# A decode kernel of grouped-query attention and an MLP on one core: weight rows of 16 and 28 KiB, the last output-weight load moved between parts of w2, and w2's first part in two transfers of 119 and 9 partitions

## The chip, the core and the metric

The kernel runs on one core of one Trainium2 chip. The metric is device time in microseconds (us), of which the median of several executions counts. One further execution was recorded with the hardware profiler; its own time is given beside its span below.

## What is computed

For a batch of 8 single tokens of width 512, the block adds the token, an attention over a cache of 8192 positions (32 query heads, 8 key/value heads), and a two-layer MLP with the Mish activation. Both branches read the same layer-normed token.

```python
def _A_ref(x, k_cache, v_cache, wq, wo):
    ...
    q = (x @ wq).reshape(B, Sq, Hq, Dh).transpose(0, 2, 1, 3)
    ...
    scores = jnp.einsum("bhqd,bhkd->bhqk", q, k) * (Dh ** -0.5)
    p = _softmax(scores, axis=-1)
    o = jnp.einsum("bhqk,bhkd->bhqd", p, v)
    return o.transpose(0, 2, 1, 3).reshape(B, Sq, Hq * Dh) @ wo

def _B_ref(x, w1, b1, w2):
    h = jnp.einsum("bsd,df->bsf", x, w1) + b1
    ...
    return jnp.einsum("bsf,fd->bsd", act, w2)

xn = _layernorm(x, axis=-1)
return x + _A_ref(xn, A_k_cache, A_v_cache, A_wq, A_wo) + _B_ref(xn, B_w1, B_b1, B_w2)
```

All data is 32-bit floating point. The two caches are 64 loads of 4 MiB each; the weights are small beside them (wq 8 MiB, wo 8 MiB, w1 3.5 MiB, w2 3.5 MiB), and everything is read once.

## The kernel before

**The work.** The query heads are worked on in 16 packs `p` of 4 batch rows each; pack `p` belongs to key/value head `n = p // 2`. A pack has four items of keys and four of values, each with one 4 MiB load. `scores` (line 305) multiplies the queries of a pack with one key block, `maximum` and `weights` (346, 368) make the exponentials of a finished pack on ScalarE and VectorE, `values` (411) multiplies them with one value block, `merge` (442) turns the result into a column of `oT`.

**The list of items and the buffers.** Lines 630 to 647 write the work out as a list `items`: wq's first part, the keys of pack 0 with w1 between them, then keys of pack `p` and values of pack `p-1` in turn, with a part of wq or of wo now and then. Each item is a load and a generator of work. The loop at line 650 issues the load of item `i + 3` ahead of the work of item `i`. All loads go into four buffers of 32 KiB per partition (`buffer`, line 90) in rotation, so the load of item `i + 4` waits on the SyncE (SP) queue until all readers of item `i` are done. All loads are issued by SP, in list order.

**Late work.** `after(k, f)` (548) puts `f` off by `k` steps; a step (`step`, 551) is taken at each `yield` of an item's work. A key item yields four times, after 8 of its 32 matmul passes each; a value item twice; a wo item once (line 619), which is a step of its own. `merge` is put off by two steps after a value item, `outputs` (456) by three after the wo item that holds its weights. `exponents` (599) comes a step after `largest` (595). TensorE and VectorE run their instructions in the order in which the program writes them (line 663 on).

**The weights.** `load_blocks` (93) brings wq, wo and w1 with 4 KiB (wq, wo) or 3.5 KiB (w1) of contiguous memory for each row of a transfer, since each partition takes one row out of each block. `project` (235) makes the queries of two heads from a wq part, `outputs` the product of two finished heads with a wo part, which is added up over the four parts in `acc`, and `mish` (483) the whole first MLP layer. `load_w2` (130) brings w2 in three loads of 16, 8 and 4 KiB rows, each into a buffer of its own, and `down` (533) multiplies each.

**The end of the list.** The last items are the four value blocks of pack 15, wo's last part, and w2's three parts. After the last `down`, VectorE adds `acc` (line 659) and SP writes the result (660).

Of the kernel before, what the change touches and what calls it, by code (L numbers as in the profile page):

```python
# [13 lines left out]
P = 128  # L14
# [42 lines left out]
W = GK * NB // P  # L57
W4 = 4
TW = W // TG
W2R = G * FT // 2 * FP // P  # L60
FAR = 1e38

# [5 lines left out]
def kernel(  # L68
# [21 lines left out]
    def buffer():  # L90
        return kv.tile([P, NB * BW], F32, name="kv")

    def load_blocks(src, lo, n):

        _, rows, width = src.shape
        t = buffer()[:rows, : n * width].rearrange("p (j f) -> p j f", j=n)
        nc.sync.dma_start(t, src[lo : lo + n].rearrange("j p f -> p j f"))
        return t

    def batch_blocks(src, p, b):  # L100
# [2 lines left out]
        return src[lo : lo + NB]  # L103

    def load_batch(src, p, b):

        t = buffer()
        nc.sync.dma_start(
            t,
            batch_blocks(src, p, b)  # L110
            .rearrange("j p f -> (j p f)")
            .rearrange("(p f) -> p f", p=P),
        )
        return t

    def load_k(p, b):
        if p > 0:
# [7 lines left out]
        )  # L125
        return t

    w2_rows = w2.rearrange("j p f -> (j p) f").rearrange("(q i) f -> q (i f)", i=W2R)

    def load_w2(lo, hi):  # L130

        t = buffer()[:, : (hi - lo) * BW]
        nc.sync.dma_start(t, w2_rows[:, lo * BW : hi * BW])
        return t

    x_sb = const.tile([B, D], F32, name="x_sb")
    nc.scalar.dma_start(x_sb, x)
# [27 lines left out]
    far = const.tile([P, NH], F32, name="far")  # L165

    isel = const.tile([P, W4], F32, name="isel")
    qT = [const.tile([P, PB * (QB + 1)], F32, name=f"qT{i}") for i in range(QBUFS)]
    qc = const.tile([P, 4, KR, REP, B], F32, name="qc")
    qc0 = const.tile([P, KA, REP, B], F32, name="qc0")  # L170
    xnT = const.tile([P, CC, B], F32, name="xnT")
    acc = const.tile([P, P], F32, name="acc")
    aT = const.tile([P, 2 * W2R, Q], F32, name="aT")

    def setup():
        make_identity(nc, ident)
        nc.gpsimd.memset(ones, 1.0)
        for t in qT:
            nc.gpsimd.memset(t, 0.0)
        nc.vector.memset(M, 0.0)  # L180
        nc.vector.memset(H, 0.0)
        for o in O:
            nc.vector.memset(o, 0.0)
# [18 lines left out]
        nc.vector.tensor_scalar(xc, xc, st[:, 4:5], None, op0=ALU.mult)  # L202
        for c in range(CC):
            nc.tensor.transpose(  # L204
                M[:, c * B : (c + 1) * B], xc[:, c * P : (c + 1) * P], ident[:B, :B]
            )
        nc.vector.tensor_copy(xnT.rearrange("p c b -> p (c b)"), M[:, : CC * B])  # L207
# [5 lines left out]
        nc.vector.reduce_sum(bsel, ident.rearrange("p (j i) -> p j i", j=NB), axis=AX.X)  # L213
        nc.vector.reduce_sum(rsel, ident.rearrange("p (g r) -> p r g", g=G), axis=AX.X)
# [13 lines left out]
        nc.vector.reduce_sum(far, mine.rearrange("p h s -> p s h"), axis=AX.X)  # L228
        nc.vector.tensor_scalar(far, far, FAR, -FAR, op0=ALU.mult, op1=ALU.add)

    q_at = [H[:, 384:512], H[:, 256:384]]

    def project(n, w):

        for c in range(CC):
            for h in range(REP):
                lo = (n % 2 * REP + h) * DH
                nc.tensor.matmul(  # L240
                    q_at[n % 2][Q * h : Q * h + B, :],
                    xnT[:, c, :],
                    w[:, c, lo : lo + DH],
                    start=(c == 0),
                    stop=(c == CC - 1),
                )

    def spread_q(n, k, copies, dst):
# [188 lines left out]
                op1=ALU.add,  # L437
            )

    oT = {}  # L440

    def merge(p, b):

        n, hb = divmod(p, NP)
        at = 168 + b * REP
        nc.tensor.matmul(M[:, at : at + REP], OS.pop((p, b)), hsel, start=True, stop=True)  # L446
        if b == PB - 1:
            if hb == 0:
                oT[n] = work.tile([P, REP, B], F32, name="oT", bufs=4)
            nc.vector.tensor_mul(  # L450
                oT[n][:, :, hb * PB : (hb + 1) * PB],
                M[:, 168 : 168 + REP * PB].rearrange("p (b h) -> p h b", h=REP),
                RT.pop(p),
            )

    def outputs(n, w):

        if n == 0:

            for g in range(G):  # L460
                nc.tensor.matmul(
                    M[Q * g : Q * g + B, 256:384],
                    ident[:B, :B],
                    x_sb[:, g * P : (g + 1) * P],
                    start=True,
                    stop=False,
                )
        for h in range(2 * REP):
            for g in range(G):
                at = h % 2 * D + g * P  # L470
                nc.tensor.matmul(  # L471
                    M[Q * g : Q * g + B, 256:384],
                    oT[n + h // REP][:, h % REP, :],
                    w[:, h // 2, at : at + P],
                    start=(h == 0 and n > 0),
                    stop=(h == 2 * REP - 1),
                )
        if n == 0:
            nc.vector.tensor_copy(acc, M[:, 256:384])
        else:  # L480
            nc.vector.tensor_add(acc, M[:, 256:384], acc)

    def mish(w1_sb):

# [6 lines left out]
        for c in range(CC):  # L491
            for g in range(G):
                nc.tensor.matmul(
                    hp[Q * g : Q * g + B, :],
                    xnT[:, c, :],
                    w1_sb[:, c * 2 + g // 2, g % 2 * FG : (g % 2 + 1) * FG],
                    start=False,
                    stop=(c == CC - 1),
                )

        scratch = work.tile([P, TG, NH, P], F32, name="e", bufs=1).rearrange("p t s f -> p (t s f)")
# [29 lines left out]
        nc.vector.transpose(aT.rearrange("p j q -> p (j q)"), act)  # L531

    def down(lo, hi, w):
        for j in range(2 * lo, 2 * hi):
            for g in range(G):
                at = (j - 2 * lo) * D + g * P
                nc.tensor.matmul(
                    H[Q * g : Q * g + B, :P],
                    aT[:, j, :B],
# [19 lines left out]
    def wq_item(i):  # L559
# [17 lines left out]
                after(2, then)  # L577
            yield

        return lambda: load_blocks(wq, i * CC, CC), work_on  # L580

    def w1_work(t):
        mish(t)
# [39 lines left out]
    def w2_work(lo, hi):  # L623
        def work_on(t):
            down(lo, hi, t)
            yield

        return work_on

    setup()  # L630
    items.append(wq_item(0))
    for i in range(PB * PACKS + PB):
        p, b = divmod(i, PB)
        if p < PACKS:
# [1 line left out]
            if b == 2 and p % (2 * NP) == 2 and p < PACKS - NP:  # L636
                items.append(wq_item(p // (2 * NP) + 1))
            if i == 2:
                items.append((lambda: load_blocks(w1, 0, 2 * CC), w1_work))
# [74 lines left out]
```

## Time and profile before

| what | value |
|---|---|
| median of 3 executions | 1320.84 us (1320.44 to 1321.55) |
| time of the profiled execution | 1319.99 us |
| span of the profiled execution, first to last instruction | 1318.2 us |
| time outside that span | 1.8 us |
| mean granted TensorE clock | 0.973 |
| memory read | 561.01 MB |

The profile gives the busy time of each engine over the span. PE is TensorE's matmul, PEld its weight load, DVE VectorE, ACT ScalarE, POOL GpSimd, SP SyncE, which only issues transfers here. A matmul of this kernel's 32-bit data is two passes, and each pass is one record, so 32 matmuls appear as "x64". In the view of windows, the columns are the stretch in us, its length, the busy time and instruction count of PE, PEld, DVE, ACT and POOL, the granted clock, the mean busy share of the 16 DMA engines, and the rate in GB/s. A packet is counted where it ends, so short windows can show a share over 1. In the timeline, the columns are start, duration, engine, line and operation, tiles, and count, and at the end the idle time before with what ended it. L328 is line 328 of the kernel before.

### The profile page before, as it was taken

To read this page: it belongs to the slowest core of one execution; us is meant where nothing else is said; L and a number is where in the kernel's file an instruction comes from. 1 tells how busy PE (TensorE), PEld (TensorE's weight loads), DVE (VectorE), ACT (ScalarE), POOL (GpSimd) and SP (SyncE) were. 2 spreads that over 40 slices of the span, in tenths; PEclk is the share of its full clock that TensorE was granted. 3 is DMA by queue.
4 is the path that set the end of the run, shared out by engine and by line. 5 is a ranking of instruction groups with operands and counts; after the bars stand their busy time and mean duration, and the time that the engine had idled before them with its cause. 6 is when DMAs were issued, how large, how long until landed. Compare 5 with 4: busy or idle time off the path is not lost.

```text
span 1318.2 us, 11315 instructions
## 1 busy us (share of the span) xinstructions
PE 1196.0 (91%) x5100; PEld 512.6 (39%) x5100; DVE 268.6 (20%) x667; ACT 42.2 (3%) x71; POOL 8.7 (1%) x10
## 2 busy tenths in 40 slices
PE   4999989999979998999998999899999899999986
PEld 3333344433434434434333434444343343343322
DVE  5330311303021031120302112131120301202021
ACT  1000000000000000000000000000000000000000
POOL 2000000000000000000000000000000000000000
PEclk9999989999989998999998999899999899999988
DMA  9999999999999999999999999999999999999997
GB/s 385 433 432 432 431 429 429 429 429 430 433 426 432 433 425 431 431 433 430 432 432 427 432 431 425 433 428 430 432 431 425 426 435 433 428 432 429 429 433 310
DMA packets 24856, 561.81 MB, mean 426 GB/s; under 512 B 2268, under 2 KB 2400, under 8 KB 7656
## 3 DMA queue, kind: packets, MB, share of 16 engines
q1 hardware_dynamic: 24784, 561.06, 99.4%
q8 instruction: 40, 0.66, 0.2%
q14 instruction: 8, 0.07, 0.0%
q10 hardware_dynamic: 24, 0.02, 0.0%
HBM read 561.01 MB, written 0.07 MB: 426 GB/s over the span
## 4 chain that ended last, share of the span: by engine, by line
PE 53%; DMA 46%; DVE 1%; issue 0%; ACT 0%
DMA kv<-in_kT 42%; PE s L328 42%; PE o L419 6%; DMA kv<-in_v 2%; PE h L263 1%; DMA kv<-in_w 1%; PE s L315 1%; PE m L471 1%; DVE e L190 0%; PE m L446 0%; PE h L240 0%; DVE qs L253 0%; DMA x_sb<-in_x 0%; PE m L372 0%; DVE oT L450 0%
## 5 line engine op out<-in xcount | busy, mean ns | idle before, releaser
L328 PE MATMUL s<-kv,qT 128*128 128x512 f32 x1920 | 873.4, 609 | 75.9 <-DMA kv<-in_kT 75.9
L328 PEld LDWEIGHTS s<-kv,qT 128*128 128x128 f32 x1920 | 361.4, 194 | 525.6 <-issue 447.2
L419 PE MATMUL o<-kv,pt 128*32 128x512 f32 x2048 | 243.3, 610 | 12.5 <-DVE pt L391 6.3
L429 DVE TENSOR_SCALAR os<-o,isel 128x128 f32<-128x128 f32 x64 | 22.5, 351 | 595.1 <-PE o L419 595.1
L419 PEld LDWEIGHTS o<-kv,pt 128*32 128x32 f32 x2048 | 73.5, 139 | 157.8 <-issue 140.4
L382 ACT ACTIVATE e<-s,nms 128x1024 f32<-128x1024 f32 x32 | 35.4, 1110 | 1182.4 <-DVE nms L376 1182.4
L391 DVE STREAM_TRANSPOSE pt<-e 128x1024 f32<-128x1024 f32 x32 | 63.0, 2006 | 39.5 <-ACT e L382 39.5
L431 DVE SCALAR_TENSOR_TENSOR os<-o,isel,os 128x128 f32<-128x128 f32 x192 | 67.4, 351 | 6.8
L339 DVE TENSOR_REDUCE nm<-s 128x1 f32<-128x1024 f32 x16 | 19.6, 1225 | 206.3 <-PE s L328 204.8
L446 PEld LDWEIGHTS m<-hsel,os 128*128 128x128 f32 x128 | 23.8, 193 | 39.4 <-issue 30.0
L315 PE MATMUL s<-kv,qT 128*64 128x512 f32 x128 | 29.9, 625 | 1.6 <-issue 1.4
L288 DVE TENSOR_SCALAR qT<-qc,bsel 128x128 f32<-128x128 f32 x120 | 30.6, 341 | 0.0
L446 PE MATMUL m<-hsel,os 128*128 128x4 f32 x128 | 19.5, 223 | 6.5 <-DVE nr L350 4.9
L263 PE MATMUL h<-psel,qs 128*128 128x32 f32 x136 | 20.4, 309 | 4.0 <-DVE qs L253 4.0
L263 PEld LDWEIGHTS h<-psel,qs 128*128 128x128 f32 x136 | 20.4, 232 | 7.7 <-DVE qs L253 4.7
L315 PEld LDWEIGHTS s<-kv,qT 128*64 128x64 f32 x128 | 9.8, 145 | 20.8 <-issue 19.8
L270 DVE COPY qc<-h 128x256 f32<-128x256 f32 (+1 forms) x9 | 3.7, 410 | 56.1 <-PE h L263 56.1
L204 PE MATMUL m<-ident,e 8*128 8x8 f32 x4 | 0.6, 247 | 12.4 <-DVE e L202 12.4
L253 DVE TENSOR_SCALAR qs<-h 128x1024 f32<-128x1024 f32 (+1 forms) x9 | 10.4, 1160 | 2.9 <-PE h L240 2.9
L450 DVE TENSOR_TENSOR oT<-m,r 128x16 f32<-128x16 f32 x16 | 2.7, 171 | 36.4 <-PE m L446 36.4
L407 DVE RECIPROCAL r<-m 128x16 f32<-128x16 f32 x16 | 4.1, 257 | 29.1 <-PE m L403 29.1
L240 PE MATMUL h<-kv,xnT 128*8 128x128 f32 x256 | 9.4, 309 | 0.3 <-DVE xnT L207 0.3
(85 smaller groups left out, 127.3 us busy)
## 6 DMA issues: line engine op xcount, KB each, us to landing
kv<-in_kT SPq DMA_DIRECT2D x64, 4096.0 KB, 24.5
kv<-in_v SPq DMA_DIRECT2D x64, 4096.0 KB, 29.6
kv<-in_wq SPq DMA_DIRECT2D x4, 2048.0 KB, 19.3
kv<-in_wo SPq DMA_DIRECT2D x4, 2048.0 KB, 20.0
kv<-in_w SPq DMA_DIRECT2D x1, 3584.0 KB, 36.3
kv<-in_w SPq DMA_DIRECT2D x1, 2048.0 KB, 21.8
kv<-in_w SPq DMA_DIRECT2D x1, 1024.0 KB, 16.4
kv<-in_w SPq DMA_DIRECT2D x1, 512.0 KB, 7.1
```

Source lines behind the costliest of these rows:

```text
L263: nc.tensor.matmul(H[:, r * R : (r + 1) * R], qs[:, r].rearrange("p g i -> p (g i)"), psel.rearrange("p h b -> p (h b)"), start=True, stop ...
L288: nc.vector.tensor_scalar(t[:, :, :, lo : lo + R - U + 1 : U], q, bsel[:, j : j + 1], None, op0=ALU.mult)
L315: nc.tensor.matmul(sp[WK * z : WK * (z + 1), cols], t[:, w : w + WK], k[:, z, at : at + 512], start=(b == 0 and i == 0), stop=(b == PB - 1 ...
L328: nc.tensor.matmul(sp[:, cols], t[:, w : w + P], k[:, at : at + 512], start=(b == 0 and r == 0), stop=(b == PB - 1 and r == KR - 1),)
L339: nc.vector.tensor_reduce(NM[p], sp, axis=AX.X, op=ALU.max, negate=True)
L382: nc.scalar.activation(e[:, :, s, :], S[p % 2].rearrange("p (t f) -> p t f", t=TG), AF.Exp, bias=nms[:, s : s + 1], accum_out=l[:, s : s + 1],
L391: nc.vector.transpose(pt.rearrange("p (m t r) -> p t m r", m=TW, t=TG)[:, half * i : half * (i + 1)], e.rearrange("p t s (q m) -> p t m (s ...
L419: nc.tensor.matmul(o[Q * c : Q * (c + 1), :], PT[p][:, W4 * R * j + b : W4 * R * (j + 1) : PB], vt[:, 512 * j : 512 * (j + 1)], start=(k = ...
L429: nc.vector.tensor_scalar(os, o[:, :DH], isel[:, 0:1], None, op0=ALU.mult)
L431: nc.vector.scalar_tensor_tensor(os, o[:, DH * i : DH * (i + 1)], isel[:, i : i + 1], os, op0=ALU.mult, op1=ALU.add,)
L446: nc.tensor.matmul(M[:, at : at + REP], OS.pop((p, b)), hsel, start=True, stop=True)
L471: nc.tensor.matmul(M[Q * g : Q * g + B, 256:384], oT[n + h // REP][:, h % REP, :], w[:, h // 2, at : at + P], start=(h == 0 and n > 0), st ...
```

## The change

Six things are changed together.

1. wq, wo and w1 are read as one flat array cut into 128 rows, so that a partition takes 16 KiB (wq, wo) or 28 KiB (w1) of contiguous memory. The rows of the weights then stand on other partitions, and the other factor of each product is brought into the same order: for wq by a strided transpose of the normed token, for w1 by a widened copy `xw` made in the set-up (two VectorE copies, eight transposes, two masked copies), for wo by a new function `turn`, which picks every fourth row of `oT` with eight small matmuls and copies the result to `oW`.
2. `mish` has 8 instead of 4 rounds over the contraction, each of the same width.
3. A wo item other than the last takes no step of its own any more: `after(3, ...)` stands, but the `yield` behind it is gone.
4. w2 has one buffer for all its parts, which are 10, 14 and 4 KiB of each row (columns 0 to 5, 5 to 12, 12 to 14 in units of 2 KiB).
5. The first of these parts is two transfers, over partitions 0 to 118 and over 119 to 127.
6. wo's last load stands between w2's first and second part; its product is put off by one step only, adds into the same PSUM region as `down`, and needs no VectorE addition of its own.

```diff
+    def rows_of(blocks):
+        return blocks.rearrange("j p f -> (j p f)").rearrange("(p f) -> p f", p=P)
+    def load_rows(blocks):
+        src = rows_of(blocks)
+        t = buffer()[:, : src.shape[1]]
+        nc.sync.dma_start(t, src)
+        return t
...
+    W2_PARTS = ((0, 5), (5, 12), (12, 14))
+    FEW = 119
+    w2_sb = []
+    def load_w2(parts):
+        if not w2_sb:
+            w2_sb.append(buffer()[:, : W2R * BW])
+        for lo, hi in parts:
+            cols = slice(lo * D, hi * D)
+            for rows in [slice(0, FEW), slice(FEW, P)] if lo == 0 else [slice(0, P)]:
+                nc.sync.dma_start(w2_sb[0][rows, cols], rows_of(w2)[rows, cols])
+        return w2_sb[0]
...
+        wide = scratch[:B, 2 * D : 2 * D + W1R * P]
+        for t in range(2):
+            nc.vector.tensor_copy(
+                wide.rearrange("b (r c t i) -> b r c t i", r=W1R, c=CC, t=2)[:, :, :, t, :],
+                xc.rearrange("b (c i r) -> b r c i", c=CC, r=W1R),
+            )
+        for r in range(W1R):
+            nc.tensor.transpose(
+                M[:, 64 + r * B : 64 + (r + 1) * B], wide[:, r * P : (r + 1) * P], ident[:B, :B]
+            )
+        for t in range(2):
+            nc.vector.tensor_scalar(xw[:, :, t, :], ..., half[:, t : t + 1], None, op0=ALU.mult)
...
+            if hb == NP - 1:
+                after(1, lambda: turn(n))
+
+    def turn(n):
+        if n % 2 == 0:
+            oW[n] = work.tile([P, OR, 2, B], F32, name="oW")
+        to = oW[n - n % 2]
+        o = oT.pop(n)
+        for k in range(2):
+            j = n % 2 * 2 + k
+            for r in range(OR):
+                nc.tensor.matmul(
+                    M[Q * j : Q * (j + 1), 384 + r * 2 * B : 384 + (r + 1) * 2 * B],
+                    ident[:, r::OR],
+                    o[:, 2 * k : 2 * k + 2, :].rearrange("p h b -> p (h b)"),
+                    start=True, stop=True,
+                )
+        rows = slice(n % 2 * 64, n % 2 * 64 + 64)
+        nc.vector.tensor_copy(
+            to[rows].rearrange("p r h b -> p (r h b)"), M[rows, 384 : 384 + OR * 2 * B]
+        )
...
     def wo_work(n):
         def work_on(t):
-            after(3, lambda: outputs(n, t))
-            yield
+            if n == HKV - 2:
+                after(1, lambda: outputs(n, t))
+                yield
+            else:
+                after(3, lambda: outputs(n, t))
...
-            if i > PB and (i - PB + 1) % (2 * NP * PB) == 0:
-                n = (p - 1) // NP - 1
-                items.append((lambda n=n: load_blocks(wo, n * 2, 4), wo_work(n)))
-    for lo, hi in ((0, 4), (4, 6), (6, 7)):
-        items.append((lambda lo=lo, hi=hi: load_w2(lo, hi), w2_work(lo, hi)))
+            if i > PB and (i - PB + 1) % (2 * NP * PB) == 0 and p < PACKS:
+                items.append(wo_item((p - 1) // NP - 1))
+    for part in W2_PARTS:
+        items.append((lambda part=part: load_w2([part]), w2_work([part])))
+        if part is W2_PARTS[0]:
+            items.append(wo_item(HKV - 2))
```

`project`, `outputs`, `mish` and `down` index the loaded rows by round instead of by block; `project`, `outputs` and `down` keep their number of matmuls in all.

More of the change, by code (lines that the diff above doesn't have):

```diff
@@ L59 @@
 TW = W // TG
+QR = CC
+OR = 4
+W1R = 2 * CC * P // P
 W2R = G * FT // 2 * FP // P
@@ L105, in load_batch @@
     def load_batch(src, p, b):
[L107 to L114, printed above, removed]
+        return load_rows(batch_blocks(src, p, b))
     def load_k(p, b):
@@ L167 @@
     isel = const.tile([P, W4], F32, name="isel")
+    half = const.tile([P, 2], F32, name="half")
     qT = [const.tile([P, PB * (QB + 1)], F32, name=f"qT{i}") for i in range(QBUFS)]
@@ L170 @@
     qc0 = const.tile([P, KA, REP, B], F32, name="qc0")
[L171 removed]
+    xnT = const.tile([P, QR, B], F32, name="xnT")
+    xw = const.tile([P, W1R, 2, B], F32, name="xw")
     acc = const.tile([P, P], F32, name="acc")
@@ L202, in setup @@
         nc.vector.tensor_scalar(xc, xc, st[:, 4:5], None, op0=ALU.mult)
[L203 to L207, printed above, removed]
+        for r in range(QR):
+            nc.tensor.transpose(M[:, r * B : (r + 1) * B], xc[:, r::QR], ident[:B, :B])
+        nc.vector.tensor_copy(xnT.rearrange("p r b -> p (r b)"), M[:, : QR * B])
         nc.vector.tensor_copy(
@@ L229, in setup @@
         nc.vector.tensor_scalar(far, far, FAR, -FAR, op0=ALU.mult, op1=ALU.add)
+        wide = scratch[:B, 2 * D : 2 * D + W1R * P]
[9 more added lines that the diff above has]
+        for t in range(2):
+            nc.vector.tensor_scalar(
+                xw[:, :, t, :],
+                M[:, 64 : 64 + W1R * B].rearrange("p (r b) -> p r b", r=W1R),
+                half[:, t : t + 1],
+                None,
+                op0=ALU.mult,
+            )
     q_at = [H[:, 384:512], H[:, 256:384]]
     def project(n, w):
-        for c in range(CC):
+        for r in range(QR):
             for h in range(REP):
-                lo = (n % 2 * REP + h) * DH
+                at = r * BW + (n % 2 * REP + h) * DH
                 nc.tensor.matmul(
                     q_at[n % 2][Q * h : Q * h + B, :],
[L242 to L245, printed above, removed]
+                    xnT[:, r, :],
+                    w[:, at : at + DH],
+                    start=(r == 0),
+                    stop=(r == QR - 1),
                 )
@@ L454, in merge @@
             )
+            if hb == NP - 1:
[12 more added lines that the diff above has]
+                    o[:, 2 * k : 2 * k + 2, :].rearrange("p h b -> p (h b)"),
+                    start=True,
+                    stop=True,
+                )
+        rows = slice(n % 2 * 64, n % 2 * 64 + 64)
+        nc.vector.tensor_copy(
+            to[rows].rearrange("p r h b -> p (r h b)"), M[rows, 384 : 384 + OR * 2 * B]
+        )
     def outputs(n, w):
+        last = n == HKV - 2
+        to = H[:, :P] if last else M[:, 256:384]
         if n == 0:
@@ L467, in outputs @@
                 )
[L468 to L477, printed above, removed]
+        for r in range(OR):
+            for h in range(2):
+                for g in range(G):
+                    at = r * BW + h * D + g * P
+                    nc.tensor.matmul(
+                        to[Q * g : Q * g + B, :],
+                        oW[n][:, r, h, :],
+                        w[:, at : at + P],
+                        start=(r == 0 and h == 0 and 0 < n and not last),
+                        stop=(r == OR - 1 and h == 1 and not last),
+                    )
         if n == 0:
-            nc.vector.tensor_copy(acc, M[:, 256:384])
-        else:
-            nc.vector.tensor_add(acc, M[:, 256:384], acc)
+            nc.vector.tensor_copy(acc, to)
+        elif not last:
+            nc.vector.tensor_add(acc, to, acc)
     def mish(w1_sb):
@@ L490, in mish @@
             )
-        for c in range(CC):
+        for r in range(W1R):
             for g in range(G):
+                at = r * F // 2 + g % 2 * FG
                 nc.tensor.matmul(
                     hp[Q * g : Q * g + B, :],
-                    xnT[:, c, :],
-                    w1_sb[:, c * 2 + g // 2, g % 2 * FG : (g % 2 + 1) * FG],
+                    xw[:, r, g // 2, :],
+                    w1_sb[:, at : at + FG],
                     start=False,
-                    stop=(c == CC - 1),
+                    stop=(r == W1R - 1),
                 )
@@ L533, in down @@
     def down(lo, hi, w):
-        for j in range(2 * lo, 2 * hi):
+        for j in range(lo, hi):
             for g in range(G):
-                at = (j - 2 * lo) * D + g * P
+                at = j * D + g * P
                 nc.tensor.matmul(
@@ L617, in work_on, with w2_work, wo_item @@
         def work_on(t):
-            after(3, lambda: outputs(n, t))
-            yield
+            if n == HKV - 2:
[3 more added lines that the diff above has]
+                after(3, lambda: outputs(n, t))
         return work_on
-    def w2_work(lo, hi):
+    def w2_work(parts):
         def work_on(t):
-            down(lo, hi, t)
-            yield
-        return work_on
+            for lo, hi in parts:
+                down(lo, hi, t)
+                yield
+        return work_on
+    def wo_item(n):
+        return lambda: load_rows(wo[n * 2 : n * 2 + 4]), wo_work(n)
     setup()
```

20 lines of the change are left out of this document (6 added, 14 removed).

## The prediction, made before the change was run

> **What bounds the kernel now.** First the busy times and queues of the page.
>
> ```profile
> span 1318.2 us, 11315 instructions
> PE 1196.0 (91%) x5100; PEld 512.6 (39%) x5100; DVE 268.6 (20%) x667; ACT 42.2 (3%) x71; POOL 8.7 (1%) x10
> q1 hardware_dynamic: 24784, 561.06, 99.4%
> q8 instruction: 40, 0.66, 0.2%
> q10 hardware_dynamic: 24, 0.02, 0.0%
> ```
>
> SP's queue keeps the 16 DMA engines busy for 99.4% of the span: the stream of loads is the limit, PE's 91% is not. Only what shortens the stream, interrupts it, or stands behind its last byte counts. Next the windows of the stream and of its end.
>
> ```profile
> 29.50:36.00 6.50, 5.11 (x17) 2.01 (x18) 3.26 (x13) 0.00 (x0) 0.00 (x0) 1.00 1.03 406
> 39.50:55.50 16.00, 16.00 (x98) 4.98 (x96) 2.30 (x5) 1.86 (x2) 0.00 (x0) 1.00 1.01 429
> 174.50:177.50 3.00, 3.00 (x9) 1.33 (x8) 0.00 (x0) 0.00 (x0) 0.00 (x0) 1.00 1.02 410
> ...
> 1304.00:1305.00 1.00, 1.00 (x8) 0.17 (x4) 0.00 (x0) 0.00 (x0) 0.00 (x0) 0.62 1.03 430
> 1305.00:1306.50 1.50, 1.16 (x12) 0.14 (x4) 0.26 (x1) 0.00 (x0) 0.00 (x0) 1.00 0.56 235
> 1312.50:1313.00 0.50, 0.50 (x28) 0.50 (x20) 0.00 (x0) 0.00 (x0) 0.00 (x0) 1.00 0.19 74
> 1313.00:1314.00 1.00, 1.00 (x44) 1.00 (x40) 0.00 (x0) 0.00 (x0) 0.00 (x0) 1.00 0.00 0
> ```
>
> w1's 3.5 KiB rows come at 406 GB/s, wq's 4 KiB rows at 410, pack 0's 16 KiB rows at 429. At 1305.0 the busy share falls from 1 to 0.56: 9 engines work, 7 have run dry, about 1305.1. The last stops near 1312.9, having had w2's last 0.5 MB (1.3 us at 410 GB/s) to do, which the seven still lacked. So **seven engines are 1312.9 - 1.3 - 1305.1 = 6.5 us ahead** of the last. The instruction row fits: 40 packets of 16.5 KB at 0.2% of 16 x 1318 us are at least 1 us of an engine each; shared by nine they make 4.4 delays, 1.5 us each if they make the 6.5.
>
> Last the timeline behind the last value load.
>
> ```profile
> 1299.68 3.65 PE L419 MATMUL o<-kv,pt 128*32 128x512 f32 x16 [4.02 <-DMA kv<-in_v]
> 1303.77 2.38 PE L419 MATMUL o<-kv,pt 128*32 128x512 f32 x16
> ...
> 1308.22 0.17 DVE L450 TENSOR_TENSOR oT<-m,r 128x16 f32<-128x16 f32 x1 [0.48 <-PE m L446]
> 1309.68 1.93 PE L537 MATMUL h<-kv,aT 128*8 128x128 f32 x64 [1.49 <-DMA kv<-in_w]
> ...
> 1312.15 1.06 PE L537 MATMUL h<-kv,aT 128*8 128x128 f32 x32 [0.54 <-DMA kv<-in_w]
> ...
> 1313.02 1.93 PE L471 MATMUL m<-kv,oT 128*8 128x128 f32 x64
> ...
> 1314.77 0.62 PE L537 MATMUL h<-kv,aT 128*8 128x128 f32 x16
> ...
> 1315.46 0.29 DVE L659 TENSOR_TENSOR res<-h,acc 128x128 f32<-128x128 f32 x1
> ```
>
> PE starts on the last value block at 1299.68, 0.45 us behind its last byte (estimated from 1312.9 and the next start); call that byte X = 1299.2. The final addition starts 16.3 us after X, with `outputs` (1.75 us) standing behind the last load.
>
> **The change part by part**, against the profiled execution's 1319.99 us (span plus 1.8), which lies 0.85 under the median.
>
> *Rows.* 2.10 MB take 5.11 us at 410 GB/s and 4.89 at 429: 0.22 saved on each of seven loads ahead of X (wo's last is counted below), and w1's 3.67 MB 9.04 against 8.55. Together **-2.0**; rates of so short windows allow -1.3 to -2.6.
>
> *Set-up.* PE waits for the new transposes before `project`.
>
> ```profile
> 11.79 0.47 DVE L202 TENSOR_SCALAR e<-e,st 8x512 f32<-8x512 f32 x1
> 12.41 0.56 PE L204 MATMUL m<-ident,e 8*128 8x8 f32 x4 [12.41 <-DVE e L202]
> 13.25 3.60 PE L240 MATMUL h<-kv,xnT 128*8 128x128 f32 x64 [0.28 <-DVE xnT L207]
> 14.56 0.17 DVE L229 TENSOR_SCALAR far<-far 128x2 f32<-128x2 f32 x1
> 16.91 23.72 SPq L120 DMA_DIRECT2D kv<-in_kT  x2
> 47.89 3.19 PE L493 MATMUL h<-kv,xnT 128*8 128x448 f32 x32
> ...
> 51.15 0.34 SPq L108 DMA_DIRECT2D kv<-in_v  x1
> ...
> 0.00:46.00 46.00, 27.95 (x168) 16.77 (x170) 17.24 (x43) 3.49 (x5) 7.75 (x9) 1.00 0.97 398
> ```
>
> DVE is free at 14.9 (one more small reduction), two strided copies of 8x512 at 0.6 each (0.47 is the nearest row; 1.0 at most) and eight transposes at 0.14 let `project` start at 17.2: +4.0. The fourth key load, issued at 40.3, waits for the first block's scores and goes to 44.3. By 46.0 the queue moved 18.3 of the 18.35 MB issued before it, so it runs dry at 46.1, or 45.4 with the faster rows; with 1.5 us from issue to full stream this costs **+0.4** (0 to 1.2). `mish` doubles its 32 passes, 3.2 us more; the value load behind its buffer goes from 51.15 to 58.4, and the two loads ahead of it last until 45.8 + 19.5 = 65.3, which hides it; without that cover it would cost the 3.2. The two masked copies lie beside `project`.
>
> *The lost step.* This decides. Three wo items no longer take their step, so `outputs` stands behind 24 passes of the next key block, not 16, and with it the wo buffer's release and the value load waiting for it on SP, with all loads behind that.
>
> ```profile
> 390.71 10.13 PE L328 MATMUL s<-kv,qT 128*128 128x512 f32 x16 [3.91 <-DMA kv<-in_kT]
> 403.10 0.33 SPq L108 DMA_DIRECT2D kv<-in_v  x1
> ...
> 713.33 9.25 PE L328 MATMUL s<-kv,qT 128*128 128x512 f32 x16 [3.97 <-DMA kv<-in_kT]
> 724.50 0.33 SPq L108 DMA_DIRECT2D kv<-in_v  x1
> ...
> 1035.94 10.07 PE L328 MATMUL s<-kv,qT 128*128 128x512 f32 x16 [3.93 <-DMA kv<-in_kT]
> 1047.94 0.33 SPq L108 DMA_DIRECT2D kv<-in_v  x1
> ...
> 1047.50:1051.50 4.00, 4.00 (x27) 1.87 (x15) 0.29 (x1) 0.00 (x0) 0.00 (x0) 1.00 0.93 369
> ...
> 313.03 0.28 PE L446 MATMUL m<-hsel,os 128*128 128x4 f32 x2
> 313.58 0.22 PE L372 MATMUL m<-ident,nx 1*128 1x1 f32 x1 [0.27 <-DVE oT L450]
> 313.73 10.57 PE L328 MATMUL s<-kv,qT 128*128 128x512 f32 x24
> ...
> L419 PEld LDWEIGHTS o<-kv,pt 128*32 128x32 f32 x2048 | 73.5, 139 | 157.8 <-issue 140.4
> 26.36 3.62 PE L263 MATMUL h<-psel,qs 128*128 128x32 f32 x16 [1.65 <-DVE qs L253]
> ```
>
> The block's landing ends PE's wait; two 4 MiB loads are then queued, 19.5 us at 429. So the last engine runs dry at landing - 0.45 + 19.5: at 409.8, 732.4 and 1055.0; the early ones sooner by their lead. Already today the third place starves them: 369 GB/s in four us is 0.56 us of all engines, 1.3 of seven. Now the issue comes later by: 8 passes, 3.5 (24 in 10.57); the merge and the transpose of line 372, until now in PE's wait, 0.7 (313.03 to 313.73); and `turn`'s 16 passes. For 32-column weights no row has this pace; between 0.03 each (line 471) and 0.226 (line 263), near the 0.139 of a weight load of this width of which part overlaps, I take 0.075: 1.2. **Later by 5.4** (4.7 to 7.8). At the third place today the seven are dry 6.5 ahead of 1055.0, at 1048.5, and 1.3 later is 1049.8, 1.8 behind the issue; with the 1.5 taken above I use 1.7. So the load streams at 410.2, 731.6, 1055.05: the last engine loses **+0.5** at the first and third place together. But all early engines wait there, and their lead goes to nothing three times. Then each stretch counts for itself: at one fetch in 33 us, 12, 20 and 7 fetches fall before, between and behind the first and third place, at most 2, 3 and 1 on one engine where uncut 39 gave 5: one delay more on the path, **+1.5** (0 to 3).
>
> *The end.* X moves by -2.0 + 0.4 + 0.5 + 1.5 = +0.4. The seven are then one delay ahead, 1.5. I read the 119 rows as 17 on each of seven engines (119 = 7 x 17; the 24 packets of q10 are 12 rows and 12 completions, so transfers of 8 and 4 rows ran on 8 and 4 engines) and the seven as the early ones. An engine moves 26.8 GB/s (429/16): 18 rows of 10 KiB 6.9, wo 4.9, 14 KiB rows 4.3, so w2's second part lands at X - 1.5 + 16.1 = X + 14.6, and PE's 0.45 + 56 passes (1.5) + 16 (0.7) end at X + 17.25: **+1.0** against 16.3. PE's own chain (values 6.5, to oT 2.2, `turn` and copy 1.75, `outputs` 1.75, `down` 2.2) ends at X + 14.85 and is hidden. The other moves are free: SP issues one transfer more, long before it is needed, and the addition into `acc` was hidden behind PE.
>
> Sum: +0.4 + 1.0 = +1.4 or 1321.4; by the median **1322.2**, own range 1320.0 to 1324.5.
>
> [...]
>
> **The rivals.**
>
> *The lead survives* (0.28): `outputs` comes no later, or the load does not hang on it. X moves by -1.6; w2's second part lands by X + 10.4, PE's chain ends at X + 14.85, -1.4: -3.0, **1317.8**. For it: the 6.5 us lead that the 18 rows would just use up. Against it: each of the three issues follows the end of `outputs` at once.
>
> *`turn` is slow* (0.22), the slower side: at 0.226 a pass it takes 3.6, the issue comes later by 7.8, and the last engine loses 2.8, 1.6 and 2.5 at the three places: 6.9 for 0.5, **1328.6**; at 0.15 a pass 3.4, **1325.1**. It decides from 0.05 a pass, where the first place starts to stall.
>
> *119 rows spread evenly* (0.07): w2's first part takes 3.1, the end comes at X + 14.9, 2.35 sooner than in the forecast: **1319.9**.
>
> *The seven are not the early ones* (0.08): a late engine carries the 18 rows, 1.5 later: **1323.7**.
>
> *One engine carries all 119* (0.02): 45.5 us instead of 6.9: **1361**.
>
> **How the numbers follow.** The forecast itself has 0.33. About 0.2% (2.6 us) is what a measurement can tell here: faster is the first rival (0.28); same is the forecast without its upper tail (0.30), the even split and half of the late seven (0.41 in all); slower the rest (0.31). For 8 in 10 the range goes from under the first rival, 1317.0, to the middle of the slow `turn`, 1325.5.
>
> **What would show it.** Windows near 405, 727 and 1050 with the rate down for all engines, the SP issues there 18 us behind PE's start on the block, not 12; no window at the end with 7 engines idle for long before the last byte. If the rate holds at the three places and PE waits for nothing behind the last value block, the first rival holds. `turn`'s 16 passes are read off directly.

## The result and the profile after

The changed kernel takes 1334.37 us (median of 5 executions, 1333.57 to 1334.87); beside it the kernel before took 1320.98 us. The ratio is 1.010, with a 95% interval of 1.0088 to 1.0111: 13 us slower, where 1322.2 was forecast and the range ended at 1325.5. The profiled execution took 1334.4 us, 14.4 more than that of before.

The first rows are from the page of the changed kernel.

```profile
span 1332.6 us, 11661 instructions
PE 1205.3 (90%) x5268; PEld 520.7 (39%) x5268; DVE 271.4 (20%) x679; ACT 42.1 (3%) x71; POOL 8.7 (1%) x10
...
GB/s 399 424 430 431 430 427 434 429 431 430 431 430 415 425 429 435 428 433 428 432 425 414 427 436 427 434 427 429 432 430 432 406 430 434 429 429 433 428 428 181
...
q1 hardware_dynamic: 20816, 561.06, 99.0%
```

The SP queue still keeps the engines busy for 99.0% of the span, now of a longer one, and moves the same 561.06 MB. So something made the same bytes take longer. The 40 slices say where: 415, 414 and 406 GB/s in slices 13, 22 and 32 (the three output items), and 181 instead of before's 310 in the last. Now the timeline behind the last value block.

```profile
1303.48 3.65 PE L447 MATMUL o<-kv,pt 128*32 128x512 f32 x16 [5.79 <-DMA kv<-in_v]
...
1318.87 2.32 PE L593 MATMUL h<-kv,aT 128*8 128x128 f32 x40 [8.79 <-DMA kv<-in_w]
...
1321.98 0.94 PE L496 MATMUL m<-oT,ident 128*32 128x16 f32 x16 [0.27 <-DVE oT L478]
...
1323.50 3.06 PE L526 MATMUL h<-kv,oW 128*8 128x128 f32 x64 [0.59 <-DMA kv<-in_wo]
...
1327.72 2.15 PE L593 MATMUL h<-kv,aT 128*8 128x128 f32 x72 [1.16 <-DMA kv<-in_w]
1329.94 0.29 DVE L723 TENSOR_TENSOR res<-h,acc 128x128 f32<-128x128 f32 x1 [6.75 <-PE h L593]
```

PE starts on the last value block 3.8 us later than before (1303.48 against 1299.68), and from there to the final addition 26.46 us pass instead of 15.78. PE sits idle for 8.79 us ahead of the first `down` (L593) and waits for w2's first part, which lands 15 us behind the value block. These 3.8 and 10.7 us make up the 14.4. The windows of that stretch follow; the last two columns are the busy share of the 16 DMA engines and the rate.

```profile
1296.00:1300.00 4.00, 1.70 (x16) 0.31 (x8) 1.40 (x4) 0.00 (x0) 0.00 (x0) 1.00 1.02 368
1300.00:1304.00 4.00, 0.52 (x4) 0.21 (x8) 0.00 (x0) 0.00 (x0) 0.00 (x0) 0.75 0.96 219
1304.00:1308.00 4.00, 4.00 (x22) 1.11 (x18) 0.00 (x0) 0.00 (x0) 0.00 (x0) 0.50 1.03 208
1308.00:1312.00 4.00, 2.08 (x16) 0.34 (x8) 1.40 (x4) 0.00 (x0) 0.00 (x0) 0.90 1.04 176
1312.00:1316.00 4.00, 0.00 (x0) 0.00 (x0) 0.00 (x0) 0.00 (x0) 0.00 (x0) 0.53 0.95 175
1316.00:1318.00 2.00, 0.00 (x0) 0.00 (x0) 0.00 (x0) 0.00 (x0) 0.00 (x0) 0.50 0.92 291
```

From 1300 to 1316 all 16 engines are busy (0.95 to 1.04) and yet move 175 to 219 GB/s. A busy engine then does 219 / (16 x 0.96) = 14.3 GB/s, and from 1308 on only 176 / (16 x 1.04) = 10.6, where the prediction had 26.8. This is not seven engines with much to do beside nine that are idle; it is 16 engines at half pace. The trace's packet records say the same: w2's 10 KiB rows, moved from 1298.9 to 1317.7, take 778 ns each (median), and wo's 128 rows of 16 KiB, which come from a transfer over 128 partitions, 1177 instead of the 613 of the kernel before.

### The profile page after: what moved, and what is told of

Read it like the earlier page. It is cut to its first block, busy times and chain, and to the rows that moved or that the text cites. A ratio compares the mean times of both kernels' runs of the same rounds, so it can differ in the third digit from the quotient of the medians.

```text
span 1332.6 us, 11661 instructions
## 1 busy us (share of the span) xinstructions
PE 1205.3 (90%) x5268; PEld 520.7 (39%) x5268; DVE 271.4 (20%) x679; ACT 42.1 (3%) x71; POOL 8.7 (1%) x10
## 2 busy tenths in 40 slices
DMA packets 20889, 561.82 MB, mean 422 GB/s; under 512 B 2268, under 2 KB 2400, under 8 KB 2536
## 3 DMA queue, kind: packets, MB, share of 16 engines
q1 hardware_dynamic: 20816, 561.06, 99.0%
## 4 chain that ended last, share of the span: by engine, by line
PE 60%; DMA 38%; DVE 1%; issue 0%; ACT 0%; SPq 0%; ACTq 0%
PE s L356 45%; DMA kv<-in_kT 35%; PE o L447 8%; DMA kv<-in_w 3%; PE s L343 2%; PE h L291 1%; PE h L549 0%; PE m L496 0%; PE m L526 0%; PE m L474 0%; DVE e L200 0%; PE h L268 0%; PE m L400 0%; DVE qs L281 0%; DMA x_sb<-in_x 0%
## 5 line engine op out<-in xcount | busy, mean ns | idle before, releaser
L367 DVE TENSOR_REDUCE nm<-s 128x1 f32<-128x1024 f32 x16 | 19.6, 1224 | 211.4 <-PE s L356 210.3
L593 PE MATMUL h<-kv,aT 128*8 128x128 f32 x112 | 4.5, 323 | 9.9 <-DMA kv<-in_w 9.9
```

Of the source, the lines that this page charges most:

```text
L367: nc.vector.tensor_reduce(NM[p], sp, axis=AX.X, op=ALU.max, negate=True)
```

## The experiments

**Theory A**: the transfer over 119 partitions slows every engine as long as it runs. **Rival B**: the slow stretch comes from something else at the end (the new rows, the order of the last loads), and the split costs only the 18 rows on seven engines at full pace.

### Taking the two suspects away, one at a time

Run e1_one_part undoes only the split:

```diff
-            for rows in [slice(0, FEW), slice(FEW, P)] if lo == 0 else [slice(0, P)]:
+            for rows in [slice(0, P)]:
```

> The changed kernel, but w2's first part is one transfer over all 128 partitions. Theory A (the transfer over 119 partitions slows every engine as long as it runs): the slow stretch at the end is gone; the last value block is 2.1 us later than in the kernel before, as the third output load left it, w2's second part lands 12.2 us behind it and the chain of PE needs 14.85, so about 0.7 over the kernel before: 1321.7 us (1320.5 to 1323.5), packets of 10 KiB at 385 ns. Rival B (the slow stretch comes from the other rows or from the order of the last loads, and the split costs only what the 18 rows on seven engines cost at full pace, 2.4 us): 1332 us, packets of 10 and 16 KiB still slow.

Measured: 1320.44 us (1319.57 to 1321.32), ratio to the kernel before 0.9994 (0.9985 to 1.0003): 0.1 us below theory A's range, and far under rival B. Windows of e1_one_part:

```profile
1300.00:1304.00 4.00, 2.12 (x16) 0.56 (x16) 0.00 (x0) 0.00 (x0) 0.00 (x0) 0.85 0.98 414
1304.00:1308.00 4.00, 4.00 (x46) 1.70 (x46) 0.33 (x1) 0.00 (x0) 0.00 (x0) 0.72 1.02 428
1308.00:1312.00 4.00, 2.87 (x78) 2.37 (x70) 1.47 (x6) 0.00 (x0) 0.00 (x0) 1.00 0.98 415
```

The same bytes, in the same order, to the same places, and the rate is twice that of the changed kernel at the same share. Its 10 KiB rows take 388 ns, the 16 KiB rows 614. The timeline of e1_one_part:

```profile
1301.88 2.83 PE L447 MATMUL o<-kv,pt 128*32 128x512 f32 x16 [3.99 <-DMA kv<-in_v]
...
1307.42 1.26 PE L593 MATMUL h<-kv,aT 128*8 128x128 f32 x40
...
1311.13 1.93 PE L526 MATMUL h<-kv,oW 128*8 128x128 f32 x64 [0.32 <-DVE oW L504]
1314.38 2.15 PE L593 MATMUL h<-kv,aT 128*8 128x128 f32 x72 [1.32 <-DMA kv<-in_w]
1316.60 0.29 DVE L723 TENSOR_TENSOR res<-h,acc 128x128 f32<-128x128 f32 x1 [5.53 <-PE h L593]
```

PE waits for nothing ahead of the first `down` now, the final addition stands 14.72 us behind the start on the last value block, and that block itself comes 1.6 sooner. The 119 rows had slowed it too: from 1290 on, single value rows took up to 2524 ns in the changed kernel, at most 1224 here.

Run e2_step_back undoes only the lost step, and e3_both undoes both:

```diff
                 after(3, lambda: outputs(n, t))
+                yield
```

> The changed kernel with the step of the three output items put back; the split stays. Theory A: the three stalls go and the seven engines keep their lead, worth 2 to 3.5 us ahead of the last value block, but the slow stretch stays: 1331.3 us (1330 to 1333). Rival B (a lead of 6.5 us takes up the 18 rows, as the first rival of the prediction had it): 1318 to 1321 us.

> The changed kernel with the step put back and w2's first part in one transfer. Theory A: the last value block lands 1.6 us sooner than in the kernel before, and 14.85 us of PE's chain stand behind it: 1318 us (1317 to 1319.5). Rival B: the slow stretch of the end stays, 1328 us or more.

Measured: e2_step_back 1333.54 us (1333.10 to 1335.60), ratio 1.0096 (1.0079 to 1.0113); e3_both 1318.21 us (1317.73 to 1319.45), ratio 0.9977 (0.9967 to 0.9986). Theory A had 1331.3 (to 1333), which e2_step_back misses by 0.5 us, and 1318.0. With the lead kept, w2's first rows start 7 us sooner (1292.1) and still end at 1316.1, and PE starts on the last value block at 1304.71, later than in the changed kernel: a lead didn't help engines that run at half pace. Without the split the lost step is worth 1320.44 - 1318.21 = 2.2 us; with it 0.8 us, where the ranges overlap. The rest of the change together is a gain, 2.8 us by e3_both. Its timeline:

```profile
1298.80 2.77 PE L447 MATMUL o<-kv,pt 128*32 128x512 f32 x16 [4.03 <-DMA kv<-in_v]
...
1308.05 1.93 PE L526 MATMUL h<-kv,oW 128*8 128x128 f32 x64 [0.32 <-DVE oW L504]
1311.12 2.15 PE L593 MATMUL h<-kv,aT 128*8 128x128 f32 x72 [1.14 <-DMA kv<-in_w]
1313.35 0.29 DVE L724 TENSOR_TENSOR res<-h,acc 128x128 f32<-128x128 f32 x1 [5.35 <-PE h L593]
```

### The split alone, in the kernel before

```diff
-        nc.sync.dma_start(t, w2_rows[:, lo * BW : hi * BW])
+        for rows in [slice(0, 119), slice(119, P)] if lo == 0 else [slice(0, P)]:
+            nc.sync.dma_start(t[rows], w2_rows[rows, lo * BW : hi * BW])
```

> The kernel before, and nothing changed in it but that w2's first load (16 KiB rows) is two transfers, over 119 partitions and over 9. Theory A: every engine is slow while it runs, 10 us over the kernel before (5 to 16), 1331 us. Rival B: 18 rows of 16 KiB are 11.0 us on seven engines at full pace, 6.1 more than 8 rows, against a lead of 6.5 us: no change, within 1 us of the kernel before.

Measured: 1337.71 us (1337.06 to 1337.94), ratio 1.0122 (1.0107 to 1.0137): 16.7 us more, just past theory A's 5 to 16 and far from rival B's 1. No other part of the change is needed for the loss, and the split of 16 KiB rows here lost more than that of 10 KiB rows in the changed kernel (13.9). Windows of e4_before_split:

```profile
1300.00:1304.00 4.00, 2.05 (x12) 0.60 (x16) 0.00 (x0) 0.00 (x0) 0.00 (x0) 0.50 0.85 204
1304.00:1308.00 4.00, 3.80 (x26) 0.82 (x18) 0.13 (x1) 0.00 (x0) 0.00 (x0) 0.81 0.85 176
```

### Why it slows: few engines, or rows in another engine's place

Theory A now splits. **A1**: in a transfer over 128 partitions each engine writes partitions of its own; where the count of rows gives an engine other partitions, two push into one place, and both go at half pace. **A2**: a transfer that uses few engines is slow, wherever it writes. Both are suppositions: the packet records name no engine and no partition. How many engines a transfer uses is estimated from its packets of 4 bytes, taken as one for each engine: 8 and 4 in the two transfers of 8 and 4 rows (q10), 16 in each of the 141 transfers on SP's queue in the kernel before, and 16 for the 119 and the 9 rows together (2256 packets on that queue in both kernels, for 141 and 142 transfers), so 7 and 9, which divide the rows as the others do. Two runs move the split of the changed kernel (`FEW = 112`, `FEW = 64`); 112, 64 and 16 rows can be divided by 16, so both are estimated to keep all 16 engines, though no count of these two runs shows it.

> The changed kernel with its split at 112 and 16 rows instead of 119 and 9. Both are multiples of 16, so that by the count of rows all 16 engines can share them (112 = 16 x 7). Theory A1 (what slows is that rows are written by another engine than the one that writes these partitions in a transfer over 128 partitions, so that two engines push into one place at a time): 7 rows an engine instead of 8 don't fit either, so slower than with one part by up to the whole loss: 1325 us (1321.5 to 1334). Theory A2 (what slows is a transfer on few engines): as with one part, 1320.4 us (1319.5 to 1321.5).

> The changed kernel with its split at 64 and 64 rows, four on each of 16 engines. Theory A1: each half reaches half of the places that 128 partitions reach, so w2's first 1.31 MB go at half the rate, 6.1 us instead of 3.1, and the end is 3 us later: 1323.5 us (1322 to 1328). Theory A2: all engines take part, so as with one part, 1320.4 us (1319.5 to 1321.5). [...]

Measured: e5_112 1326.45 us (1325.08 to 1327.33), ratio 1.0038 (1.0023 to 1.0053); e7_64 1325.45 us (1324.52 to 1328.29), ratio 1.0035 (1.0023 to 1.0047). A2 had 1320.4 for both; both lie in A1's ranges. One window each, of e5_112 and then of e7_64:

```profile
1300.00:1304.00 4.00, 0.47 (x4) 0.21 (x8) 0.00 (x0) 0.00 (x0) 0.00 (x0) 0.87 0.93 201
```

```profile
1300.00:1304.00 4.00, 0.40 (x4) 0.22 (x8) 0.00 (x0) 0.00 (x0) 0.00 (x0) 0.55 0.95 224
```

Again all engines are busy (0.93 and 0.95), at half the rate (201 and 224 GB/s). An even half is hardly better than 112 rows; that 64 rows reach half of the places is A1's supposition, and no run shows it. The stretch is shorter than with 119 rows: from 1308 to 1312 the rate is 363 and 417 GB/s, where the changed kernel has 176. By the estimate above each engine has 8 rows here and up to 18 there.

The two runs that decide write the same rows of w2 to two sets of partitions, 64 apart, in eight transfers of seven rows: by A2 both are slow alike, by A1 the place can make one slow and not the other. The packets under 512 B put seven engines on such a transfer, by the estimate above (2324 in e8_extra_own, 2268 in the changed kernel: 56 more for the eight). The labels say which set was taken for the engines' own; no run shows that. The runs add to e3_both, ahead of w2's first part (`base` is 0 in one, 64 in the other):

```diff
+            for i in range(4):
+                for half in (0, 32):
+                    lo = base + half + i
+                    nc.sync.dma_start(
+                        qT[0][lo : lo + 28 : 4, : 5 * D], rows_of(w2)[half + i : half + i + 28 : 4, : 5 * D]
+                    )
```

> The kernel with the step put back and w2's first part in one transfer (1318.2 us), and ahead of that part eight more transfers of 7 rows of 10 KiB, whose data nobody reads: 8 rows on each of seven engines. [...] The rows are 3.1 us on seven engines which are 6.5 us ahead. Theory A1: hidden, 1318.2 us (1317.7 to 1319.5), packets at 385 ns. Theory A2: 8/17 of the slow stretch of the 119 rows, 5 to 7 us: 1324 us, packets of 10 KiB at twice their time.

> As the run before, with the same rows read, but written 64 partitions further up: by theory A1 into the partitions of seven other engines. Theory A1: those places get 8 rows of 10 KiB more, at least 3.1 us of one engine's pace, and the engines that share them slow each other: 1323 us (1321.3 to 1326), packets well over 385 ns while they run. Theory A2: the same time as the run before, 1324 us by it, and the same packets.

Measured: e8_extra_own 1322.90 us (1321.96 to 1324.56), ratio 1.0013 (1.0003 to 1.0022); e9_extra_other 1326.64 us (1326.20 to 1327.61), ratio 1.0043 (1.0028 to 1.0057). The same window of e8_extra_own and of e9_extra_other, while the extra rows move:

```profile
1292.00:1296.00 4.00, 2.07 (x18) 0.63 (x17) 1.40 (x4) 0.00 (x0) 0.00 (x0) 1.00 0.75 317
```

```profile
1292.00:1296.00 4.00, 1.31 (x15) 0.17 (x4) 1.40 (x4) 0.00 (x0) 0.00 (x0) 1.00 0.80 166
```

A busy engine moves 317 / (16 x 0.75) = 26.4 GB/s in the first and 166 / (16 x 0.80) = 13.0 in the second. In the packet records the first 49 extra rows take 385 to 392 ns in the first run. In the second, 21 of the 28 that start by 1296.2 take 700 to 825, and value rows of 32 KiB, which move at the same time, up to 2569 instead of 1216; PE starts on the last value block at 1301.88 instead of 1299.63. From 1300.4 on, when the value block is all but in, 16 of the 17 extra rows left take 385 to 393 again. So these partitions aren't slow in themselves; the rows were slow while value rows moved too. In the first run transfers of seven rows slowed neither themselves (385 to 392 ns) nor the value rows (at most 1216), so A2 falls; the same rows sent to other partitions slowed both, as A1 has it.

The time of e8_extra_own missed its 1318.2 for a reason of the experiment. Its waits of SP, and two rows of its timeline:

```profile
SPq L139 <- DMA kv<-in_v: 24.6, 3, 9.0
```

```profile
1299.61 0.69 SPq L139 DMA_DIRECT2D qT<-in_w  x1
...
1300.40 0.38 SPq L145 DMA_DIRECT2D kv<-in_w  x1
```

SP waited three times for value blocks to land before it could issue extra transfers; the eighth went only when the last value block had landed, and w2 stood behind it on SP, so the stream ran dry (46 GB/s from 1298 to 1300). e9_extra_other has the same hold, so the two can be set against each other, at 3.7 us apart, but not against e3_both: whether the extra rows by themselves would have been hidden, the time doesn't show.

No run shows which partitions an engine writes, in a transfer over 128 or over 119. That the place decides is measured (26.4 against 13.0 GB/s a busy engine for the same rows); that two engines push into one place is inferred.

### The other parts

Four runs tried the rest: three with edits to e3_both (the last of them on top of the first), and the lost step alone in the kernel before.

f1_setup_order moves the widened copy for w1:

```diff
-    setup()
+    widen = setup()
...
                 spread(1)()
+                widen()
```

> The kernel with the step put back and w2's first part in one transfer (1318.2 us), and in it the widened copy for w1 (two wide copies, eight transposes, two masked copies) moved behind project and the spreading of the first queries. By the prediction's working the set-up costs 0.4 us because the fourth key load is issued 4 us later; the trace of the changed kernel shows the last engine 0.9 us later behind it. Expected: 0.4 to 0.9 sooner, 1317.6 us (1317.2 to 1318.2). Rival (the engines that lose there are not those that end last): no change, 1318.2 us.

Measured: 1319.09 us (1317.83 to 1320.38), ratio 0.9984 (0.9975 to 0.9993): no gain, and outside the expected range. SP's first key loads in e3_both, then in f1_setup_order (start, and length from the first of the two to the end of the second):

```profile
20.35 22.52 SPq L119 DMA_DIRECT2D kv<-in_kT  x2
```

```profile
16.96 26.94 SPq L119 DMA_DIRECT2D kv<-in_kT  x2
```

The third load goes 3.4 us sooner, but the fourth ends its issue at 43.9 instead of 42.9: the eight transposes now stand in front of the first scores, for which that load waits. The wait was moved, not taken away.

f2_before_no_step drops the `yield` behind the first three output items of the kernel before.

> The kernel before, and nothing changed in it but that the first three output items take no step. The value load behind them is issued 4.2 us later by the prediction's working (8 passes 3.5, merge and transpose 0.7; there is no turn here). At the first place 407.3 and at the third 1052.1, ahead of the 409.8 and 1055.0 at which the last engine runs dry, so only the early engines wait. The prediction's theory (a lead that is cut lets each stretch count for itself): 1 us more, 1322.1 us (1321.3 to 1323.6). Rival (only a stall of the last engine costs): 1321.1 us, no change.

Measured: 1321.71 us (1320.53 to 1323.36), ratio 1.0006 (0.9997 to 1.0015). Its value loads go at 407.13 and 1052.41, as worked out, but the interval holds both a cost of 1 us and none: inconclusive.

f3_wo_first puts wo's last load back ahead of w2, with `after(3, ...)` and its own addition.

> The kernel with the step put back and w2's first part in one transfer (1318.2 us), with wo's last load and its addition where the kernel before had them, ahead of all w2. The final addition stood 16.3 us behind the last value byte in the kernel before and 15.0 in that kernel (1313.35 against 1298.35). If the new place of wo makes that difference: 1.3 us more, 1319.5 us (1319 to 1320). Rival (the shape of w2's parts does, or the lead): 1318.2 us.

Measured: 1321.32 us (1319.58 to 1322.28), ratio 0.9998 (0.9989 to 1.0007): some 3 us more than e3_both, not 1.3. Four of its eleven executions lie at 1319.6 to 1320.0, the others at 1321.3 to 1322.3, the profiled one among them. Its timeline:

```profile
1312.10 2.28 PE L593 MATMUL h<-kv,aT 128*8 128x128 f32 x56 [2.32 <-DMA kv<-in_w]
1314.14 3.09 PE L526 MATMUL m<-kv,oW 128*8 128x128 f32 x64
1317.05 0.62 PE L593 MATMUL h<-kv,aT 128*8 128x128 f32 x16
```

`outputs` stands behind the last wait for w2 here; in e3_both it fills part of the time before that wait. In this execution its 64 passes took 3.09 us, with the granted clock at 0.50 from 1314 to 1316, where e3_both's took 1.93 at 1.00. So the place is worth 1.9 to 3.1 us, by the pace of PE. Another 1.0 us of the difference between the two profiles stands ahead of the last value block (1299.81 against 1298.80), where the two kernels load the same.

f4_sooner keeps f1_setup_order's edit and takes `outputs` one step earlier still, with `turn` just ahead of it:

```diff
-                after(3, lambda: outputs(n, t))
+                after(2, lambda: outputs(n, t))
...
-                after(1, lambda: turn(n))
+                late.insert(0, [1, lambda: turn(n)])
```

> As the first of these four, and outputs put off by two steps instead of three at the first three output items, with turn taken just ahead of it: the value loads are issued some 3 us sooner than in the kernel before, so that no engine runs dry at the third place either, where 1.3 us of seven engines were lost. Expected by the prediction's theory of leads: 0 to 0.5 sooner than the first of these, 1317.3 us (1316.8 to 1318). Rival (PE's wait for turn's copy ahead of outputs costs): 0.5 to 1.5 more, 1318.1 to 1319.1 us.

Measured: 1317.93 us (1317.71 to 1319.37), ratio 0.9977 (0.9967 to 0.9987). That beats the kernel before by as much as e3_both does, and can't be told from it, nor clearly from f1_setup_order, on which it is built (1.2 us by the medians, the intervals overlap). The e3_both edit is the simpler one.

## Why the prediction was wrong

**The failed step is in "The end": "An engine moves 26.8 GB/s (429/16): 18 rows of 10 KiB 6.9".** The pace of an engine was taken as its own, whatever partitions it writes. w2's first part took 18.8 us from its first row to its last, with 10.6 to 14.3 GB/s a busy engine for most of it, and slowed the value block ahead of it and wo's load behind it. Instead of +1.0 the end gave +10.7, with 1.6 more ahead of the last value block (e1_one_part against the changed kernel): of the 14.4 us, the split made 13.3 by the profiles, 13.9 by the medians. None of the rivals had it. The forecast set the 18 rows against the idle engines of the end (busy share 0.56); one transfer took 1320.44 us, the splits at 119, 112 and 64 rows 1334.37, 1326.45 and 1325.45. The idle engines were seen rightly, and seven engines for the 119 rows agree with the packets of 4 bytes (16 for 119 and 9 rows together); that these rows would slow all the others was not seen.

**The assumption "the seven as the early ones" fell too.** In e8_extra_own's packet records, 28 of the first 49 extra rows have moved by 1294.8; the other 21 move from 1295.3 to 1300.9. At one row of each transfer to an engine, seven in all, that is four early engines and three late ones, an estimate, since the records name no engine. That is the rival given 0.08; its price of 1.5 us is small beside the 13 that the split cost.

**The lost step was right in place and size; half of its mechanism stays argued.** Views of the changed kernel: SP's issues, and the windows at the three places, where the kernel before had 432, 416 and 430 GB/s.

```profile
406.98 0.33 SPq L104 DMA_DIRECT2D kv<-in_v  x1
...
730.62 0.33 SPq L104 DMA_DIRECT2D kv<-in_v  x1
...
1054.49 0.33 SPq L104 DMA_DIRECT2D kv<-in_v  x1
```

```profile
403.00:411.00 8.00, 8.00 (x30) 3.52 (x30) 2.44 (x10) 0.00 (x0) 0.00 (x0) 1.00 1.01 432
724.00:732.00 8.00, 8.00 (x40) 3.55 (x34) 2.44 (x10) 0.00 (x0) 0.00 (x0) 1.00 0.97 416
1047.00:1056.00 9.00, 9.00 (x59) 4.14 (x54) 2.43 (x10) 0.00 (x0) 0.00 (x0) 1.00 1.03 430
```

```profile
403.00:411.00 8.00, 8.00 (x91) 4.21 (x93) 3.48 (x14) 0.00 (x0) 0.00 (x0) 1.00 0.86 338
724.00:732.00 8.00, 8.00 (x93) 4.72 (x93) 5.32 (x11) 0.00 (x0) 0.00 (x0) 1.00 0.88 360
1047.00:1056.00 9.00, 9.00 (x95) 4.97 (x94) 5.95 (x12) 0.32 (x2) 0.00 (x0) 1.00 0.93 373
```

The issues come 3.9, 6.1 and 6.6 us later (5.4 was forecast, 4.7 to 7.8). The first of the two groups of windows is of the kernel before, the second of the changed one: the rate falls at all three places. The price was 0.5 + 1.5 = 2.0 us by the forecast and 2.2 by e1_one_part against e3_both. That a cut lead lets each stretch count for itself, the 1.5 of it, stays argued: f2_before_no_step, which should have shown it alone, can't tell 1 us from none. `turn` costs 0.94 us for 16 passes, 0.059 each (0.075 was taken), so the slow `turn` falls.

**Rows and set-up** were forecast at -1.6 by the last value block; e3_both starts on it 0.88 us sooner, in one profile each. The delay of the set-up came as worked out: in the changed kernel `project` starts at 17.0 (17.2 forecast) and the fourth key load goes at 44.2 (44.3). The stall of the set-up shows in the first two windows below, of the changed kernel and then of the kernel before, at 377 against 418 GB/s or 0.4 us of 4, the size forecast. (The 1.5 us from issue to full stream in that forecast was an estimate; in the kernel before SP issues its first load at 0.73, and the busy share of the DMA engines is 0.60 from 2.0 to 2.5 and 1.21 from 2.5 to 3.0.) But the stall is not in every execution: the third window is of e3_both and the fourth of f3_wo_first, which load the same up to there.

```profile
44.00:48.00 4.00, 4.00 (x22) 1.51 (x20) 0.00 (x0) 0.00 (x0) 0.00 (x0) 1.00 0.92 377
```

```profile
44.00:48.00 4.00, 4.00 (x28) 1.06 (x28) 0.00 (x0) 0.00 (x0) 0.00 (x0) 1.00 0.98 418
```

```profile
44.00:48.00 4.00, 4.00 (x22) 1.51 (x20) 0.00 (x0) 0.00 (x0) 0.00 (x0) 1.00 1.01 430
```

```profile
44.00:48.00 4.00, 4.00 (x22) 1.52 (x20) 0.00 (x0) 0.00 (x0) 0.00 (x0) 1.00 0.89 340
```

SP ends the issue of the fourth key load at 42.9 in the profile of e3_both and at 45.0 in that of f3_wo_first, the one that starts on the last value block 1.0 us later. So 0.88 us is within what single executions differ by, and e3_both's profile has no stall that f1_setup_order could have taken away. Which of the two terms was off stays open. Nor is the gain of the rows shown by itself: f3_wo_first has all of them and is no faster than the kernel before.

**The tail without the split was right.** The rival of an even spread had 1319.9, and e1_one_part has 1320.44; the rival in which the lead survives had 1317.8, and e3_both, in which it does, has 1318.21. The totals agree better than the terms: by the profiles e1_one_part starts on the last value block 2.2 us later than the kernel before, where +0.4 was forecast, so part of the agreement is luck. What broke the forecast is the one transfer of a new shape, priced by rows of the old shape.

## What to carry to other kernels

Read the busy share and the rate together: a busy share near 1 at half the rate was here no lack of engines but 16 busy ones at half pace, and the rate divided by the busy engines (10.6 to 14.3 GB/s instead of 26.8) shows it in one window. None of the loads over 119, 112 or 64 partitions was a part of a full load at the same pace (219, 201 and 224 GB/s from 1300 to 1304, 414 in e1_one_part); price such a load, and all that runs beside it, as unknown until a run shows it. The idle time of some DMA engines at the end was not filled by splitting w2's first part at 119 rows, which lost 13.9 us; the gain that the runs show, 2 to 3 us by f3_wo_first against e3_both, came from moving wo's last load between the parts of w2 and its product ahead of the last landing.

## What was not expected of the hardware

A load of 1.2 MB over 119 partitions halved the pace of all 16 DMA engines for some 16 us (10.6 to 14.3 GB/s a busy engine, 26.4 in e8_extra_own), and loads issued ahead of it and behind it, over 128 partitions, ran at half pace with it (16 KiB rows at 1177 ns, 613 in the kernel before). Transfers of seven rows in steps of four partitions, from partition 0, slowed nothing (385 to 392 ns a row); 64 partitions further up, the same rows took up to 825 ns while value rows still moved, and these up to 2569 instead of 1216.
